# A convolution and a low-rank mixer on one core: the large products in halves of 64 rows

## The chip, the cores and the metric

The kernel runs on one core of a Trainium2 chip. The metric is the device time of one execution in microseconds (us); shorter is better. Engines are named as the profile names them: PE is TensorE's matmul and PEld its weight load, DVE is VectorE, ACT is ScalarE, POOL is GpSimd, SP is SyncE; "q" after a name is that engine's sequencer. L560 is line 560 of the kernel before.

## The reference

`x` is (8, 4224, 192) and `out` has the same shape, float32. The first stage is a causal convolution along the sequence with seven taps for each of eight heads of 24 channels, after a softmax of the taps. The second stage mixes.

```python
w = softmax(weight)                                  # 8 heads x 7 taps
y[b, s, h, :] = sum_k w[h, k] * xpad[b, s + k, h, :]  # x padded with 6 zeros in front
h = (y^T @ U) @ V          # U: 4224 x 32, V: 32 x 4224, along the sequence
u = y + h^T
out = u + relu(u @ w_ch1) @ w_ch2    # 192 -> 768 -> 192
```

`h` needs a whole batch of `y` before the first row of `u`.

## The kernel before, in words

The sequence of a batch is 33 tiles of 128 rows, and all batches together 264 tiles; 33 groups of eight tiles go through the mixer, one group a round. Data is bfloat16, sums in PSUM are float32.

**Convolution** (`conv_two`, L355). A 128 x 128 band matrix per head multiplies blocks of tiles, two heads into the two banks of one PSUM buffer, and ScalarE or VectorE copies them to `y_sb`. A second band brings the last rows of the tile before; batches 0 and 1 use both bands. From batch 2 on only the first band is used, and the first six rows of each tile come from `conv_halo` (L381): POOL loads the rows around each tile border (`load_halo`, L92), eight matmuls make the six rows, ScalarE copies them, and two DMAs on SP bring them to `y_sb` by way of DRAM (`put_halo`, L408).

**Low rank** (`low_rank`, L414). 33 matmuls of 32 columns of `U` each sum `y^T U` of a batch in four groups of 32 partitions; VectorE copies the sums out. `fold` (L434) is a float32 matmul (two passes) that adds the four groups and leaves the result in two places; VectorE copies it to `tt_sb`. `mix_quad` (L443) multiplies `V` with it for four tiles, lower and upper 64 rows of the array by turns into two banks, and VectorE adds `y_sb` into `u_sb` (L467). `turn_by_dma` (L540) transposes a group of `u_sb` with one DMA on SP into `uT_sb`; for groups 0 and 1 TensorE does it (`straight`, `turn`).

**The mixer's products.** `h1_chunk` (L551) is the first product: 192 channels as three blocks of 64 rows, so lower and upper half of the array hold different tiles and write different banks, six matmuls of 512 columns a chunk, six chunks a group; ScalarE (m = 0, 2, 4, 5) or VectorE (m = 1, 3) applies the relu. `w2_step` (L574) is the second: per tile six matmuls with all 128 rows and 192 columns (L582), a buffer for four tiles; VectorE adds `u_sb` (L593), and SP stores (L600).

**What sets the order.** All instructions stand in the order in which the program writes them, for each engine in its own queue. In round g come some quads of group g + 2, the six chunks of group g, the other quads, and then eight pieces of the second product, the second half of group g - 1 and the first half of group g; `beside` lists what stands after which piece: convolutions of a later batch, the transposing DMA of group g + 2 (after the third piece), `low_rank`, `fold`, the loads of a batch two ahead at a round's end. One pool of four PSUM buffers of two banks, `big`, serves all of it in turn.

The lines that need to be seen:

```python
quads = [(g + AHEAD, 0)], [(g + AHEAD, QT)]
for q in quads[0]: mix_quad(*q)
for m in range(MC): h1_chunk(g, m)
for q in quads[1]: mix_quad(*q)
...
gg, n0 = (g - 1, W2N // 2) if i < NP // 2 else (g, -W2N // 2)
```

Of the kernel before, what the change touches and what calls it, by code (L numbers as in the profile page):

```python
# [15 lines left out]
def kernel(  # L16
# [41 lines left out]
    hxs = ctx.enter_context(tc.tile_pool(name="hxs", bufs=2))  # L58
# [9 lines left out]
    big_ps = ctx.enter_context(tc.tile_pool(name="big_ps", bufs=4, space=bass.MemoryType.PSUM))  # L68

    def big(dtype=F32):  # L70
        return big_ps.tile([P, 2, BK * 4 // mybir.dt.size(dtype)], dtype, name="big")
# [4 lines left out]
    x_tiles, hx_tiles = {}, {}  # L76
    blocks_0 = [(0, 8), (8, 16), (16, 24), (24, 30), (30, NT)]
    assert blocks_0[0][1] >= GT
    blocks = [(s, min(s + CB, NT)) for s in range(0, NT, CB)]
# [12 lines left out]
    def load_halo(b):  # L92

        hx = hxs.tile([HJ * HP, HS, D], BF16, name="hx_sb")
        for s in range(HS):
            src = x[b, (s + 1) * P - HALO, :]
            nc.gpsimd.dma_start(  # L97
                out=hx[:, s, :],
                in_=bass.AP(src.tensor, src.offset, [[D, HP], [HS * P * D, HJ], [1, D]]),
            )  # L100
        hx_tiles[b] = hx
# [67 lines left out]
    halo_band = cst.tile([HJ * HP, H, P], BF16, name="halo_band")  # L169
# [5 lines left out]
    idle_ps = big()  # L175
# [31 lines left out]
    def keep_busy(n):  # L207
# [19 lines left out]
        in_=ident[0 : HJ * HP, 0:1].to_broadcast([HJ * HP, H * P]),  # L227
# [55 lines left out]
    nc.vector.memset(V_sb[:, 0 : S // 2].bitcast(U32), 0)  # L283

    fold_sb = cst.tile([P, P], F32, name="fold_sb")
    nc.gpsimd.memset(fold_sb[:], 0.0)
    id4 = ident[:].rearrange("p (q r) -> p q r", r=R)
    f2 = cst.tile([P, 2, R], F32, name="f2")
    nc.gpsimd.tensor_tensor(out=f2[:], in0=id4[:, 0:2, :], in1=id4[:, 2:4, :], op=ALU.add)
    for h in range(2):  # L290
        nc.gpsimd.tensor_tensor(
            out=fold_sb[:, h * HB : h * HB + R], in0=f2[:, 0, :], in1=f2[:, 1, :], op=ALU.add
        )
# [21 lines left out]
    def build_halo_band():  # L315
        cps = big()
        for c in range(HALO):
# [8 lines left out]
            out=halo_band[:, :, 0 : HALO * HJ].rearrange("p h (c j) -> p h c j", j=HJ),  # L326
# [9 lines left out]

    def load_others():
        first = GT * P
        nc.gpsimd.dma_start(out=V_sb[0:R, 0:first], in_=moe_V[:, 0:first])
# [5 lines left out]
        nc.gpsimd.dma_start(out=V_sb[0:R, first:], in_=moe_V[:, first:])  # L345
        nc.gpsimd.dma_start(out=V_sb[HB : HB + R, :], in_=moe_V[:])
# [6 lines left out]
    y_tiles, tps_tiles, tt_tiles, u_tiles, ut_tiles = {}, {}, {}, {}, {}  # L353
# [372 lines left out]
```

## Time and profile before

| What | Value |
|---|---|
| Runs | 342.75, 346.08 and 346.15 us, median 346.08 |
| The profiled execution | 343.05 us, of which the profile's span is 341.2 |
| TensorE granted clock | 1.000 |
| First chunk of round 0 begins | 21.82 us |
| First chunks of rounds 1, 2, 3 and 4 begin | 31.00, 47.37, 60.19 and 69.73 us |
| Last matmul of the second product ends | 337.28 us |
| First product L560 | 1188 matmuls, 133.8 us busy, 376 ns one |
| Second product L582 | 1584 matmuls, 148.6 us busy, 246 ns one |
| Its weight loads | 1584, 98 ns one |
| Relu on ScalarE L570, on VectorE L572 | 132 by 1022 ns, 66 by 1218 ns |
| o_sb on VectorE L593 | 67 by 946 ns |
| u_sb on VectorE L467 | 128 by 549 ns |

How to read it: matmuls are pipelined, so the length of one (246 ns) is longer than the distance between two starts. The chain of waits is followed back from the last instruction to what released each; a piece of it on PE is a stretch in which TensorE's own order sets the time. "Idle before" with a releaser tells what ended a wait.

### The profile page before, as it was taken

To read this page: it belongs to the slowest core of one execution; us is meant where nothing else is said; L and a number is where in the kernel's file an instruction comes from. 1 tells how busy PE (TensorE), PEld (TensorE's weight loads), DVE (VectorE), ACT (ScalarE), POOL (GpSimd) and SP (SyncE) were. 2 spreads that over 40 slices of the span, in tenths; PEclk is the share of its full clock that TensorE was granted. 3 is DMA by queue.
4 is the path that set the end of the run, shared out by engine and by line. 5 is a ranking of instruction groups with operands and counts; after the bars stand their busy time and mean duration, and the time that the engine had idled before them with its cause. 6 is when DMAs were issued, how large, how long until landed. Compare 5 with 4: busy or idle time off the path is not lost.

```text
span 341.2 us, 8411 instructions
## 1 busy us (share of the span) xinstructions
PE 329.2 (96%) x3663; PEld 232.8 (68%) x3663; DVE 224.2 (66%) x323; ACT 193.1 (57%) x220; POOL 43.7 (13%) x70
## 2 busy tenths in 40 slices
PE   4998998999999999999999999999999999999995
PEld 2856666666677777766676777776677767777775
DVE  6758574667666556776766656667677767777553
ACT  5456647676555756666555745685565434444550
POOL 7680050050005000140005000000000000000000
PEclk9999999999999999999999999999999999999999
DMA  8999999999955996599947997535247444464424
GB/s 127 198 197 193 180 151 164 221 186 192 231 162 119 200 210 174 99 207 167 255 140 134 205 200 158 170 102 161 95 138 149 140 140 138 140 140 140 139 95 138
DMA packets 122965, 55.40 MB, mean 162 GB/s; under 512 B 88266, under 2 KB 122730, under 8 KB 122794
## 3 DMA queue, kind: packets, MB, share of 16 engines
q1 hardware_dynamic: 83988, 39.31, 48.4%
q0 software_dynamic: 38896, 15.29, 37.8%
q8 instruction: 28, 0.46, 0.5%
q10 hardware_dynamic: 44, 0.27, 0.3%
q14 instruction: 9, 0.07, 0.1%
HBM read 31.56 MB, written 26.39 MB: 170 GB/s over the span
## 4 chain that ended last, share of the span: by engine, by line
PE 90%; DMA 6%; ACT 1%; DVE 1%; issue 0%; POOLq 0%
PE big L582 38%; PE big L560 36%; PE big L365 8%; PE big L455 4%; DMA uT_sb<-u_sb 4%; DMA x_sb<-in_x_dram 2%; PE big L422 2%; PE big L436 1%; PE big L192 1%; ACT rl_sb L570 1%; PE big L388 1%; DVE o_sb L593 0%; DVE u_sb L467 0%; ACT uT_sb L537 0%; PE big L526 0%
## 5 line engine op out<-in xcount | busy, mean ns | idle before, releaser
L570 ACT ACTIVATE rl_sb<-big 128x1024 bf16<-128x1024 f32 x132 | 131.6, 1022 | 92.0 <-DVE o_sb L593 35.6
L582 PE MATMUL big<-W_sb,rl_sb 128*128 128x192 bf16 x1584 | 148.6, 246 | 0.0
L582 PEld LDWEIGHTS <-rl_sb 128*128 128x128 bf16 x1584 | 130.4, 98 | 14.4 <-issue 5.7
L560 PE MATMUL big<-uT_sb,W_sb 64*128 64x512 bf16 x1188 | 133.8, 376 | 2.0 <-DMA uT_sb<-u_sb 1.4
L593 DVE TENSOR_TENSOR o_sb<-big,u_sb 128x768 f32<-128x768 f32 (+1 forms) x67 | 63.4, 946 | 84.3 <-PE big L582 84.3
L560 PEld LDWEIGHTS <-W_sb 64*128 64x128 bf16 x1188 | 58.2, 94 | 64.8 <-DVE u_sb L467 6.8
L572 DVE TENSOR_SCALAR rl_sb<-big 128x1024 bf16<-128x1024 f32 x66 | 78.1, 1218 | 4.0 <-PE big L560 3.6
L375 ACT ACTIVATE y_sb<-big 128x1008 bf16<-128x1008 f32 (+4 forms) x64 | 48.8, 769 | 36.5 <-PE big L365 35.8
L467 DVE TENSOR_TENSOR u_sb<-y_sb,big 128x384 bf16<-128x384 bf16 x128 | 64.8, 549 | 5.5 <-PE big L455 5.4
L87 POOL DMA_DIRECT2D x_sb<-in_x_dram x19 | 21.8, 1153 | 139.4 <-PE big L365 138.2
L365 PE MATMUL big<-x_sb,band_sb 128*128 128x504 bf16 (+4 forms) x208 | 38.0, 302 | 1.0 <-DMA x_sb<-in_x_dram 0.9
L455 PE MATMUL big<-tt_sb,V_sb 64*128 64x192 bf16 x264 | 22.1, 245 | 1.0 <-ACT rl_sb L570 0.6
L365 PEld LDWEIGHTS <-band_sb 128*128 128x128 bf16 x208 | 18.3, 101 | 3.0 <-ACT U_sb L203 1.0
L455 PEld LDWEIGHTS <-V_sb 64*128 64x128 bf16 x264 | 10.5, 94 | 13.6 <-issue 6.4
L97 POOL DMA_DIRECT2D hx_sb<-in_x_dram x24 | 13.7, 577 | 0.0
L377 DVE CAST y_sb<-big 128x384 bf16<-128x384 f32 (+4 forms) x12 | 6.8, 570 | 4.5 <-PE big L365 4.1
L440 DVE CAST tt_sb<-big 128x192 bf16<-128x192 f32 x8 | 2.9, 357 | 9.4 <-PE big L436 9.4
L422 PE MATMUL big<-y_sb,U_sb 128*32 128x192 bf16 x264 | 7.7, 252 | 0.0
L422 PEld LDWEIGHTS <-U_sb 128*32 128x32 bf16 x264 | 6.2, 139 | 1.2 <-issue 1.1
L397 ACT ACTIVATE hy_sb<-big 48x384 bf16<-48x384 f32 x12 | 5.2, 478 | 2.6 <-PE big L388 2.6
L436 PE MATMUL big<-tf_sb,fold_sb 128*128 128x192 f32 x16 | 4.3, 348 | 0.2 <-DVE tf_sb L431 0.2
L209 PE MATMUL big<-ident 128*128 128x512 bf16 x3 | 1.6, 617 | 2.8 <-POOL ident L129 2.8
(68 smaller groups left out, 53.2 us busy)
## 6 DMA issues: line engine op xcount, KB each, us to landing
out_dram<-o_sb SPq DMA_DIRECT2D x65, 384.0 KB, 3.3
x_sb<-in_x_dram POOLq DMA_DIRECT2D x7, 1008.0 KB, 13.4
x_sb<-in_x_dram POOLq DMA_DIRECT2D x7, 576.0 KB, 17.3
x_sb<-in_x_dram POOLq DMA_DIRECT2D x3, 384.0 KB, 7.5
W_sb<-in_moe_w_ch_dram POOLq DMA_DIRECT2D x3, 288.0 KB, 7.6
hx_sb<-in_x_dram POOLq DMA_DIRECT2D x24, 36.0 KB, 16.9
uT_sb<-u_sb SPq DMA_TRANSPOSE x31, 4.0
hy_dr<-hy_sb SPq DMA_DIRECT2D x6, 72.0 KB
```

What stands on the lines that cost most here:

```text
L87: nc.gpsimd.dma_start(out=x_tiles[b][:, 1 + s0 : 1 + s1, :], in_=x[b, s0 * P : s1 * P, :].rearrange("(j p) d -> p j d", p=P),)
L97: nc.gpsimd.dma_start(out=hx[:, s, :], in_=bass.AP(src.tensor, src.offset, [[D, HP], [HS * P * D, HJ], [1, D]]),)
L365: nc.tensor.matmul(out=cps[:, q, 0:n], lhsT=band_sb[:, hh + q, w, :], rhs=x_sb[:, 1 + s0 - w : 1 + s1 - w, hc], start=(w == 0), stop=(w == ...
L375: nc.scalar.activation(out=dst, in_=src, func=ACT.Copy)
L422: nc.tensor.matmul(out=tps[q * R : (q + 1) * R, 0, 0:D], lhsT=U_sb[:, :, j], rhs=y_sb[:, j, :], start=(j < n), stop=(j >= NT - n),)
L455: nc.tensor.matmul(out=ups[:, t, i * D : (i + 1) * D], lhsT=V_sb[rows, j * P : (j + 1) * P], rhs=tt_tiles[b][rows, :], start=True, stop=True,)
L467: nc.vector.tensor_tensor(out=dst, in0=y_tiles[b][:, j : j + 2, :].rearrange("p t (k r) -> p t k r", r=HB), in1=add, op=ALU.add,)
L560: nc.tensor.matmul(out=h1[:, q, :], lhsT=W1_sb[rows, k, m * P : (m + 1) * P], rhs=ut[rows, k, :, :], start=(k == 0), stop=(k == KB - 1),)
L570: nc.scalar.activation(out=rl, in_=src, func=ACT.Relu)
L572: nc.vector.tensor_scalar_max(out=rl, in0=src, scalar1=0.0)
L582: nc.tensor.matmul(out=ch[:, t % w, 0:D], lhsT=rl_tiles[g][:, m, t, :], rhs=W2_sb[:, m, :], start=(m == 0), stop=(m == MC - 1),)
L593: nc.vector.tensor_tensor(out=o_sb[:, 0:w, :].rearrange("p t (k r) -> p t k r", r=HB), in0=ch[:, 0:w, 0:D].rearrange("p t (k r) -> p t k r ...
```

## The change

**Halves.** A new class issues a product as two groups of sums in two banks of one buffer, in two parts. In the first part the lower 64 rows of the array work for bank 0 and the upper 64 for bank 1; in the second part they change banks. Each whole matmul becomes two with half the rows, in pairs. The second part may begin when the last two matmuls of the first have ended: a `nop` on POOL waits for these two, and the first two matmuls of the second part wait for that `nop`.

**Where it is used.** The second product (`w2_parts`), the convolutions from batch 1 on (`conv_parts`), and the halo matmuls (`halo_parts`, now with 128 rows of which 32 are zero). The last group's second product stays whole (`w2_whole`). `low_rank` stays at 128 rows. The second product of a group runs wholly in the next round, in two halves of four tiles, each from one buffer of a pool of its own (`ch_ps`, one buffer); `big` keeps three.

**No fold.** VectorE copies the upper 64 partitions of the low-rank sums and adds the lower 64 to them twice, once for each half of `tt_sb`; two of the four groups remain to be added, and `V_sb` holds `V` in all four groups of 32 partitions, so the product with `V` adds them. For group 0 the four groups are used as they are. V is loaded four times over, by POOL and one copy on SP.

**Other moves.** Batch 1 uses one band and a halo like the later ones. Blocks of x are 17 and 16 tiles (21 and 12 before). x of a batch is loaded in two steps of one round, its halo in two steps of the next.

**The order.** Each round follows a word: x0, x1 are quads of group g + 2; m0 to m5 chunks; P0 and Q0 the first and second part of the second product's first four tiles, P1 and Q1 of the others; c and d first and second parts of convolutions; h and H of the halo; L is `low_rank`, t the transposing DMA, l0 and l1 loads, s `put_halo`, y other quads, u another transposing DMA, T a transpose on TensorE, b the halo's band.

```diff
-    big_ps = ctx.enter_context(tc.tile_pool(name="big_ps", bufs=4, space=bass.MemoryType.PSUM))
+    big_ps = ctx.enter_context(tc.tile_pool(name="big_ps", bufs=3, space=bass.MemoryType.PSUM))
+    ch_ps = ctx.enter_context(tc.tile_pool(name="ch_ps", bufs=1, space=bass.MemoryType.PSUM))
...
-    blocks = [(s, min(s + CB, NT)) for s in range(0, NT, CB)]
+    blocks = [(0, (NT + 1) // 2), ((NT + 1) // 2, NT)]
...
+        def V_rows(c0, c1, n):
+            return bass.AP(moe_V.tensor, moe_V.offset + c0, [[0, n], [S, R], [1, c1 - c0]])
+        nc.gpsimd.dma_start(out=V_sb[:, 0:V1], in_=V_rows(0, V1, P // R))
...
+        nc.gpsimd.dma_start(out=V_sb[0:HB, V1:], in_=V_rows(V1, S, HB // R))
+        nc.sync.dma_start(out=V_sb[HB:, V1:], in_=V_sb[0:HB, V1:])
...
+    class Halves:
+        def __init__(self, items):
+            self.items = items
+        def part(self, second):
+            N = len(self.items[0])
+            last = []
+            for n in range(N):
+                for h, rows in enumerate((lower, upper)):
+                    out_, lhsT, rhs = self.items[h ^ second][n]
+                    mm = nc.tensor.matmul(
+                        out=out_,
+                        lhsT=lhsT[rows],
+                        rhs=rhs[rows],
+                        start=not second and n == 0,
+                        stop=bool(second) and n == N - 1,
+                    )
+                    if not second and n == N - 1:
+                        last.append(mm.ins)
+                    elif second and n == 0:
+                        tc.add_manual_dep(mm.ins, self.seen.name, SYNC, reason="a bank changes hands")
+            if not second:
+                self.seen = nc.gpsimd.nop().ins
+                for ins in last:
+                    tc.add_manual_dep(self.seen, ins.name, SYNC, reason="a bank changes hands")
...
-    def fold(b):
-        tps = tps_tiles[b]
-        nc.tensor.matmul(
-            out=tps[:, 1, 0:D], lhsT=fold_sb[:], rhs=tt_tiles[b][:], start=True, stop=True
-        )
...
+            if b == 0:
+                part = tfs.tile([P, D], BF16, name="part_sb")
+                nc.vector.tensor_copy(out=part[:], in_=tps[:, 0, 0:D])
+                part_tiles[b] = part
+            tf = tfs.tile([HB, D], F32, name="tf_sb")
+            nc.vector.tensor_copy(out=tf[:], in_=tps[HB:, 0, 0:D])
+            tt = tts.tile([P, D], BF16, name="tt_sb")
+            for h in range(2):
+                nc.vector.tensor_tensor(
+                    out=tt[h * HB : (h + 1) * HB, :], in0=tps[0:HB, 0, 0:D], in1=tf[:], op=ALU.add
+                )
...
+            ch = big(pool=ch_ps)
+            state["ch"] = ch[:].rearrange("p h (t w) -> p (h t) w", t=QT)[:, :, 0:D]
+            state["mm"] = Halves(
+                [
+                    [
+                        (
+                            ch[:, q, i * (BK // QT) : i * (BK // QT) + D],
+                            rl_tiles[g][:, m, t0 + q * QT + i, :],
+                            W2_sb[:, m, :],
+                        )
+                        for i in range(QT)
+                        for m in range(MC)
+                    ]
+                    for q in range(2)
+                ]
+            )
...
+    USUAL = "x0 m0 m1 P0 c0 m2 d0 c1 l0 Q0 d1 m3 s m4 L x1 t P1 m5 h l1 Q1 H"
+    ORDERS = {
+        0: "m0 y0 m1 y1 m2 m3 T m4 x0 m5 x1 t b",
+        1: "y0 m0 y1 m1 P0 c0 m2 d0 c1 Q0 d1 x0 m3 c2 m4 d2 P1 x1 t c3 m5 d3 c4 h Q1 H d4",
+        2: "m0 m1 P0 c0 m2 d0 c1 Q0 d1 m3 c2 m4 d2 s P1 c3 m5 Q1 d3 L",
+        3: "y0 y1 u m0 m1 P0 c0 m2 d0 c1 l0 Q0 d1 x0 m3 m4 x1 t P1 c2 m5 d2 c3 h l1 Q1 H d3",
+        4: "x0 m0 m1 P0 c0 m2 d0 c1 l0 Q0 d1 m3 m4 x1 t P1 c2 l1 m5 d2 s Q1",
+    }
...
+        last = (nb * NT) // GT - AHEAD - 1
+        if nb == 1:
+            last, shares = 2, {1: 5, 2: 3}
+        elif nb == 2:
+            shares = {2: 1, 3: 4, 4: 3}
+        else:
+            shares = {g: 2 for g in range(last - 4, last)}
...
+        for m in range(MC):
+            on_act = m not in ((2, 4, 5) if len(conv_by[g]) > 2 else (2, 4))
+            if g == 0:
+                on_act = m != 4
...
+    w2_whole(NG - 1, 0, HT, ch_ps)
+    w2_whole(NG - 1, HT, QT, big_ps)
+    w2_whole(NG - 1, HT + QT, QT, big_ps)
```

In rounds from 5 to 24 each round has two convolutions; x of batches 3 to 7 is loaded in rounds 3, 5, 9, 13 and 17, and `low_rank` of batches 1 to 7 stands in rounds 2, 5, 9, 13, 17, 21 and 25.

## The prediction

> **What bounds the kernel now.** First the page: busy shares, clock and DMA rows, and the chain that ended last.
>
> ```profile
> span 341.2 us, 8411 instructions
> PE 329.2 (96%) x3663; PEld 232.8 (68%) x3663; DVE 224.2 (66%) x323; ACT 193.1 (57%) x220; POOL 43.7 (13%) x70
> ...
> PEclk9999999999999999999999999999999999999999
> DMA  8999999999955996599947997535247444464424
> ...
> PE 90%; DMA 6%; ACT 1%; DVE 1%; issue 0%; POOLq 0%
> PE big L582 38%; PE big L560 36%; PE big L365 8%; PE big L455 4%; DMA uT_sb<-u_sb 4%; DMA x_sb<-in_x_dram 2%; PE big L422 2%; PE big L436 1%; PE big L192 1%; ACT rl_sb L570 1%; PE big L388 1%; DVE o_sb L593 0%; DVE u_sb L467 0%; ACT uT_sb L537 0%; PE big L526 0%
> ```
>
> TensorE's order of work is the time, at full clock. The DMA engines are as full in the first third, and one DMA is on the chain. So two questions: what in TensorE's order is not streaming, and which DMAs does it wait for? Next the chain in one round, in order of time (start, length, what):
>
> ```profile
> 89.63 0.27 PE big L455 x4
> 89.90 3.89 PE big L560 x36
> 93.79 0.17 PE big L455 x4
> 93.95 1.59 PE big L582 x18
> 95.55 0.24 PE big L365 x2
> 95.79 0.99 PE big L582 x12
> ```
>
> L560 streams: 18 pairs in 3.89 is 0.216 a pair. L582 streams at 0.99/12 = 0.0825. Four L455 after L560 (both in halves of 64 rows) take 0.17; after L582 (128 rows) 0.27, so that joint costs 0.105. Eighteen L582 should take 1.485 and take 1.59 after L455: 0.105 again. L365 to L582, both 128 rows, costs nothing. Then the timeline, for halves at 192 columns and for the late DMA:
>
> ```profile
> 89.56 0.12 PEld L455 LDWEIGHTS <-V_sb 64*128 64x128 bf16 x4 [0.16 <-issue]
> 89.57 0.34 PE L455 MATMUL big<-tt_sb,V_sb 64*128 64x192 bf16 x4
> 89.66 1.69 PEld L560 LDWEIGHTS <-W_sb 64*128 64x128 bf16 x18
> 89.74 4.05 PE L560 MATMUL big<-uT_sb,W_sb 64*128 64x512 bf16 x36
> ```
>
> ```profile
> 48.17 3.87 SPq L542 DMA_TRANSPOSE uT_sb<-u_sb  x1
> 60.19 4.06 PE L560 MATMUL big<-uT_sb,W_sb 64*128 64x512 bf16 x36 [1.42 <-DMA uT_sb<-u_sb]
> ```
>
> Four half matmuls start at 89.57 and the next at 89.74: two pairs in 0.17, 0.083 a pair, as fast as one whole matmul. The transposing DMA issued at 48.17 landed 12.0 later and TensorE stood 1.42. Its landing while x was loading, and with the queues empty (windows at 114 and 132 us):
>
> ```profile
> DMA to landing us min/median/max: 10.6/10.6/10.6
> ```
> ```profile
> DMA to landing us min/median/max: 3.2/3.2/3.2
> ```
>
> **The sum** is made against the profiled execution: span 341.2, own time 343.05, so 1.85 lies around it. That time is 0.9% below the median of the runs (346.08).
>
> *Removed or saved.*
> Joints: 2 x 0.105 in each of about 32 rounds, 6.7; the last group stays whole and keeps 0.2: -6.5. L422 stays at 128 rows and keeps its joints (0.89 + 0.11 a batch).
> The second product: 1,536 whole matmuls at 0.0825 become 1,536 pairs. Bounds from rows: 0.083 (L455) and 0.094 (one half's LDWEIGHTS lasts 94 ns, if it could not hide), 0 to +18. I take 0, since L582 hides a 98 ns load in 82.5 already.
> First convolutions: two matmuls of 408 columns by 0.17 either way (L365: 504 columns, 0.21 each): 0. Batch 1 gets one band instead of two: in the chain 5.4 become 2.7, its halo adds 0.34: -2.3.
> Halo in halves: 8 pairs for 8 matmuls, 0.34 a batch; if loads limit it 0.66, so 0 to +2.2; taken 0.
> Fold (L436): 0.35 in seven batches, 2.45; in the prologue, fold and tt_sb are out of the way of L504: -0.7 (L422 ends 19.17, three L488 groups until 20.05, L504 then instead of at 20.73). Together -3.2. VectorE instead makes one copy and two adds by 0.36 a batch; they stand in its queue before the next u_sb adds, counted below.
> The 1.42 wait at 60.19: that transpose now has a round and a half more: -1.4.
> V_sb's two memsets (0.94 each on VectorE) go: they lay beside the first convolutions, and a convolution copy may start sooner: 0.
> Sum: -13.4.
>
> *Added.* One round by hand, a round with low_rank and halo, from x0 = 0, with 0.165 a quad, 0.65 a chunk, 0.99 a part, 0.17 a convolution half: m0 to 0.81, m1 1.46, P0 2.45, c0 2.62, m2 3.27, d0, c1 3.61, Q0 4.60, d1, m3, m4 6.07, L 7.07, x1 7.23, P1 8.2, m5 8.9, h 9.1, Q1 10.1, H 10.3. VectorE: m2 until 4.75, o_sb 5.82, m4 7.55, L's three 8.63, x1's adds 9.7.
> Three PSUM buffers instead of four (the fourth is ch): h's buffer is read by ScalarE (2 x 0.48) from 10.5 to 11.45, and the next round's m1 wants it at 11.1: 0.38 x 6 batches, +2.3. Only one ch: in the eight rounds without convolutions P1 wants it at 5.55, when VectorE gives it up (2 o_sb by 0.96 and m2 by 1.22): +0.5. All other turns of the three buffers have 0.2 or more to spare.
> Round 0: ScalarE has five chunks by 1.02; buffers come back late at y1, m3, m5 and x1, by hand 2.45 of idle against some 1.6 now: +0.9. Batch 1: low_rank ends round 2 and y0 needs its tt_sb; three VectorE steps, 1.3 of idle against 1.0: +0.3. Round 1 has VectorE busy 9.6 of 10.6, and POOL, whose loads wait for landings of earlier ones, may hold the first bank changes until x of batch 1 has landed (31.2 now): 0.5 to 2.5, taken 1.5.
> POOL's own queue: batch 1's halo adds four issues by 0.57; x (1.05 to 1.45) and halo loads are now spread between steps, behind the nops that matter. SP: same stores, one copy of V more, under the prologue.
>
> *The wait at a bank change* (127 of them). TensorE's last matmul ends, POOL's nop sees it, the second part may start. Behind the waiting matmul stands all of TensorE. Cover: one chunk, 0.65, at the least. Of it 0.48 is left after the last matmul's end (0.65 + 0.08 - 0.25), less a weight load of 0.1: 0.38. Price: a matmul's end to ScalarE's start 0.04 (L365 to L375), VectorE's end to TensorE 0.05 (L440 to L455), a POOL instruction after the one it waits for 0.07 (L305): some 0.15. Far end: POOL's loads start 0.23 to 0.67 after L436 or L365 ended. [...] With 0.67 + 0.08 each exposed wait costs 0.37, and 63 have only a chunk as cover: +23. A wait added to a bound engine can't gain.
>
> *The transposing DMA.* Now it is issued 5.2 us into a round (95.08 against 89.90) and needed two rounds later. After the change it stands behind m4 and x1 on VectorE: issued at 9.75 of the round above, needed at 10.3 + 0.4 + 8.9 + 0.2 = 19.7: 9.95. In rounds 5, 9, 13 and 17 x loads run beside it: the first half issued at 3.95, the second at 9.4. Rows beside x loads: 10.6, 10.7, 11.5, 12.0; alone 3.2. All contended: 0.65 to 2.05 late. But the second half of x is issued only then, and a gap opens before it; the nearest row, 10.6, less some of that: I take 0.5 late, five times (round 3 too): +2.5; ends 0 and +10.
>
> Added: 2.3 + 0.5 + 0.9 + 0.3 + 1.5 + 2.5 = 8.0. Net -5.4: 337.6 in the profiled execution's terms. The runs lie up to 3.1 above that execution; I put the time at 339.0, some 1.4 up.
>
> [...] By the trace a switch between 128 and 64 rows costs 0.105, both ways. [...] By the trace four half loads start within 0.03 us and pairs follow at 0.083. [...] The rows do not show them one at a time.
>
> **Rivals.**
> (a) The sum: 337.6, own range 334 to 342. Chance 0.42.
> (b) The transposes land in time: 335 (337.6 - 2.5). For: 3.2 alone, and loads are spread. Against: every transpose beside x needed over 10. 0.22.
> (c) They are late by the worst row, 2.05 five times: +7.7, 345. For: 12.0 at 48.17. Against: the gap between the halves. 0.14.
> (d) Slower: the way through POOL outlasts the chunk. 63 exposed waits; at the far end 361. It decides from 0.54 instead of 0.38 on: 63 x 0.14 = 8.8 takes the net -5.4 to +3.4, 1%. For: POOL's 0.67. Against: every other hand-over is under 0.1. 0.14, near 350 on average.
> (e) Pairs at 0.094: 355. Against: L455. 0.08.
> That the halves don't do what they say, and the joints stay, would add 6.5 to (a), 344; the joint-free L365 to L582 speaks against; it is part of (c)'s chance.
>
> **How the numbers follow.** About 1% is what a measurement of this kernel can tell from no change: 339.6 to 346.5 in own terms. Faster: (b) 0.22 and most of (a), 0.36: 0.58. Same: the rest of (a), 0.06, and (c): 0.20. Slower: (d) and (e): 0.22. Range: from (b) with half the other stalls gone, 331, to the middle of (d), 350; beyond lies (e) and half of (d), and a little below: under 0.2.
>
> **What would show it.** Joints: the chain shows L560, quads and the second product with no step above 0.17 a quad, and parts of 24 halves in 0.99. Bank changes: no idle of TensorE put down to POOL. h: ScalarE's hy_sb ends idle before a first product's chunk, 0.4 in six rounds. Transposes: idle put down to the DMA into uT_sb in rounds 7, 11, 15 and 19. Waits after each second part would prove (d); parts of 1.1 us (e).

## The result and the profile after

The changed kernel takes 369.45 us (median of four runs, 368.15 to 378.89) against 346.0 of the kernel before: a ratio of 1.068, with an interval of 1.061 to 1.076. It is slower by 6.8%, where 339 was forecast. The run of 378.89 was disturbed and is left out of the ratio. The profiled execution took 368.68 us, of which 366.9 are its span.

The page of the kernel after, the same rows as were shown of before:

```profile
span 366.9 us, 11937 instructions
PE 326.5 (89%) x5343; PEld 243.9 (66%) x5343; DVE 231.1 (63%) x334; ACT 189.7 (52%) x221; POOL 44.8 (12%) x69
...
PE   4970488978979999988999999899999999999994
...
PEclk9995599999999999999999999999999999999999
DMA  8998996339999954999499949996445556544533
...
PE 59%; DMA 14%; DVE 2%; issue 1%; ACT 0%; ACTq 0%; DVEq 0%; SPq 0%
```

TensorE is busy for a little less time than before (326.5 us against 329.2), in a span that is 25.7 longer. The row PE has a hole from the third to the fifth slice (18 to 46 us), empty in the fourth, and in the fourth and fifth the granted clock is 5 tenths. DMAs hold 14% of the chain, where they held 6; this chain reaches back only to 89 us, so round 0 is not on it. So the products did not get slower; TensorE waits, and first of all in round 0.

The chain in a round well behind these first ones, with two convolutions, to be set beside the round shown of before (start, length, what):

```profile
116.61 1.29 PE big L642 x12
117.90 0.17 PE big L537 x4
118.07 0.99 PE big L374 x24
119.06 0.65 PE big L642 x6
119.70 0.99 PE big L374 x24
120.69 0.16 PE big L537 x4
```

A part of the second product (24 halves) takes 0.99, a chunk 0.65, a quad 0.16 or 0.17 behind a chunk and behind the second product alike. The steps of 0.105 that stood beside L582 in the kernel before are gone, and nothing waits for a bank. (Behind `low_rank`, still of 128 rows, a quad takes 0.27.) This is what the prediction drew. Now round 0, in the timeline of the kernel after:

```profile
24.38 1.23 PE L642 MATMUL big<-uT_sb,W_sb 64*128 64x512 bf16 x6 [0.26 <-ACT uT_sb L597]
34.29 0.54 SPq L344 DMA_DIRECT2D V_sb<-V_sb  x1
34.32 0.34 PE L537 MATMUL big<-tt_sb,V_sb 64*128 64x192 bf16 x1 [8.72 <-DMA V_sb<-in_moe_V_dram]
34.83 2.49 POOL L88 DMA_DIRECT2D x_sb<-in_x_dram  x2 [9.51 <-DMA V_sb<-in_moe_V_dram]
41.33 0.50 PE L537 MATMUL big<-tt_sb,V_sb 64*128 64x192 bf16 x3 [6.67 <-DMA V_sb<-V_sb]
```

The first quad waits 8.72 us for the load of V's rest, its next matmul 6.67 more for SP's copy of the same rows into the upper 64 partitions, which could only start when the load had landed (34.29). POOL's own next loads of x stand 9.51 us behind the same load. What this does to the clock is in the windows of the kernel after (stretch, length, busy time of each engine, granted clock, DMA share, GB/s):

```profile
20.00:25.30 5.30, 4.58 (x91) 3.28 (x88) 3.41 (x9) 2.17 (x6) 1.68 (x3) 1.00 1.93 156
25.30:34.30 9.00, 0.30 (x4) 0.00 (x0) 0.53 (x2) 1.02 (x1) 0.01 (x1) 0.63 1.10 139
34.30:41.40 7.10, 0.41 (x3) 0.18 (x5) 0.00 (x0) 0.00 (x0) 2.48 (x2) 0.50 1.01 137
41.40:45.00 3.60, 3.60 (x24) 2.55 (x25) 2.04 (x4) 1.28 (x2) 0.59 (x1) 0.54 1.60 192
```

TensorE is idle here from 25.61, and in the trace's own list its clock is 0.5 from 27.65 to 44.72: the windows show 0.63 and 0.50 in the wait, and the next 3.6 us of work run at 0.54. Later, the chain passes the halo rows of batch 2, which go through DRAM, while x of batch 3 is loading (its last block lands at 102.4):

```profile
89.70 10.85 DMA hy_dr<-hy_sb
100.60 6.75 DMA y_sb<-hy_dr
107.39 0.89 PE big L503 x32
```

**Where the time went.** For every matmul the trace has its start, and how long it streams; what lies between two starts beyond that is a wait. The waits of the profiled executions add up as in the table; beside them stand the time lost to the granted clock (busy time in windows of 4 us by one less the clock that the windows show, where it is under 1), and the time from the first convolution to the first low-rank matmul, less the waits in it. The last column is the span less these three: work that TensorE streams, joints included, and the two ends of the span.

| Kernel | span | waits | clock | convolutions of batch 0 | the rest |
|---|---|---|---|---|---|
| before | 341.2 | 7.5 | 0.0 | 9.2 | 324.5 |
| after | 366.9 | 40.0 | 1.9 | 12.7 | 312.4 |

The change took 12.1 us out of the work and put 32.5 into waits: V 15.7; the transposing DMAs 4.1 (1.6 before); the halo rows 3.6; u_sb of VectorE 3.4, y_sb of ScalarE 2.9, o_sb of VectorE 2.8, hy_sb 2.6 (PSUM buffers that these four free late); the rest small. The 3.5 of the fifth column will be shown not to belong to the change.

### The profile page after: what moved, and what is told of

The parts are those of the page before. It is cut to its first block, busy times and chain, and to the rows that moved or that the text cites. A ratio compares the mean times of both kernels' runs of the same rounds, so it can differ in the third digit from the quotient of the medians.

```text
span 366.9 us, 11937 instructions
## 1 busy us (share of the span) xinstructions
PE 326.5 (89%) x5343; PEld 243.9 (66%) x5343; DVE 231.1 (63%) x334; ACT 189.7 (52%) x221; POOL 44.8 (12%) x69
## 4 chain that ended last, share of the span: by engine, by line
PE 59%; DMA 14%; DVE 2%; issue 1%; ACT 0%; ACTq 0%; DVEq 0%; SPq 0%
PE big L374 29%; PE big L642 25%; DMA uT_sb<-u_sb 9%; DMA hy_dr<-hy_sb 3%; PE big L537 2%; DMA y_sb<-hy_dr 2%; DVE o_sb L661 2%; PE big L503 1%; PE big L709 1%; ACT y_sb L413 0%; ACT hy_sb L474 0%; DVE rl_sb L654 0%; ACTq L652 0%; DVEq L654 0%; SPq L490 0%
## 5 line engine op out<-in xcount | busy, mean ns | idle before, releaser
L642 PE MATMUL big<-uT_sb,W_sb 64*128 64x512 bf16 x1188 | 155.4, 379 | 8.5 <-DMA uT_sb<-u_sb 3.6
L374 PE MATMUL big<-W_sb,rl_sb 64*128 64x192 bf16 x3072 | 149.1, 243 | 0.3 <-DVE o_sb L661 0.3
L374 PEld LDWEIGHTS <-rl_sb 64*128 64x128 bf16 x3072 | 132.3, 94 | 17.8 <-issue 0.9
L654 DVE TENSOR_SCALAR rl_sb<-big 128x1024 bf16<-128x1024 f32 x69 | 84.5, 1225 | 72.1 <-PE big L642 71.1
L413 ACT ACTIVATE y_sb<-big 128x816 bf16<-128x816 f32 (+4 forms) x66 | 50.8, 770 | 46.5 <-PE big L374 37.7
L374 PE MATMUL big<-x_sb,band_sb 64*128 64x408 bf16 (+1 forms) x224 | 34.2, 328 | 0.3
L374 PEld LDWEIGHTS <-band_sb 64*128 64x128 bf16 x224 | 12.6, 94 | 7.1 <-DVE u_sb L549 0.9
L399 PE MATMUL big<-x_sb,band_sb 128*128 128x192 bf16 (+2 forms) x80 | 10.9, 328 | 0.8 <-DMA x_sb<-in_x_dram 0.8
L399 PEld LDWEIGHTS <-band_sb 128*128 128x128 bf16 x80 | 9.6, 141 | 1.6 <-ACT U_sb L207 0.9
L520 DVE TENSOR_TENSOR tt_sb<-big,tf_sb 64x192 bf16<-64x192 f32 x16 | 5.6, 350 | 0.4
```

The costliest lines, as they stand in the source:

```text
L374: mm = nc.tensor.matmul(out=out_, lhsT=lhsT[rows], rhs=rhs[rows], start=not second and n == 0, stop=bool(second) and n == N - 1,)
L399: nc.tensor.matmul(out=cps[:, q, 0:n], lhsT=band_sb[:, hh + q, w, :], rhs=x_tiles[b][:, 1 + s0 - w : 1 + s1 - w, hc], start=(w == 0), stop ...
L413: nc.scalar.activation(out=dst, in_=src, func=ACT.Copy)
L642: nc.tensor.matmul(out=h1[:, q, :], lhsT=W1_sb[rows, k, m * P : (m + 1) * P], rhs=ut[rows, k, :, :], start=(k == 0), stop=(k == KB - 1),)
L654: nc.vector.tensor_scalar_max(out=rl, in0=src, scalar1=0.0)
```

## The experiments

My theory was that the load of V, as it is written, is the main cost: one DMA whose source repeats V's 32 rows by an outer step of zero. That the form makes it slow was an estimate, from the landing at 34.27 us. In transfers of 32 rows I expected V's rest by 14, TensorE's two waits in round 0 (the first for the load, the second for SP's copy) under 2 us together, no cut of the clock behind them, and 351 to 355 for the kernel. Rivals: the bytes (V four times over), SP's copy alone, or loads that collide whatever form V has. Ratios are to the kernel before, with their intervals.

**V by groups of 32 rows.**

```diff
-        nc.gpsimd.dma_start(out=V_sb[:, 0:V1], in_=V_rows(0, V1, P // R))
+        for n in range(P // R):
+            nc.gpsimd.dma_start(out=V_sb[n * R : (n + 1) * R, 0:V1], in_=moe_V[:, 0:V1])
...
-        nc.gpsimd.dma_start(out=V_sb[0:HB, V1:], in_=V_rows(V1, S, HB // R))
+        for n in range(HB // R):
+            nc.gpsimd.dma_start(out=V_sb[n * R : (n + 1) * R, V1:], in_=moe_V[:, V1:])
```

> The kernel after, with only the load of V written differently: instead of one transfer whose source repeats V's 32 rows by an outer step of zero (4 x 32 rows, then 2 x 32), one transfer for every group of 32 rows (four, then two); bytes, queue and SP's copy stay. [...] Rival 1, the bytes (V is read four times over, 0.8 MB in place of 0.5): the load still lands after 25 us, time 366 or more. Rival 2, SP's copy from SBUF to SBUF is slow whatever comes before it (6.99 us): the first wait goes, the second stays, about 360.

Measured: 365.77, ratio 1.055 (1.050 to 1.061), where 351 to 355 was expected. The transfers are quicker, the time hardly. V's rest lands at 22.5 us instead of 34.27, but not by 14: its two transfers are issued at 14.8 and 15.5, and their packets begin at 17.5. From issue to landing of V's transfers in this kernel (13.7, 19.6 and 25.5 in the kernel after):

```profile
DMA to landing us min/median/max: 5.7/7.9/8.7
```

The wait for the load is gone and 3.5 us are left behind SP's copy, as rival 2 had it in part; V's 15.7 have become 3.5. But other waits and the clock took most of it back. Groups of the kernel with V by rows:

```profile
L644 PE MATMUL big<-uT_sb,W_sb 64*128 64x512 bf16 x1188 | 158.0, 384 | 9.6 <-DMA uT_sb<-u_sb 5.7 <-DVE u_sb L551 1.1 <-ACT hy_sb L476 0.6
L505 PE MATMUL big<-y_sb,U_sb 128*32 128x192 bf16 x264 | 8.7, 266 | 5.0 <-DMA y_sb<-hy_dr 4.7 <-ACT y_sb L415 0.4
```

and its windows:

```profile
96.00:100.00 4.00, 0.23 (x3) 0.07 (x2) 1.23 (x1) 0.52 (x1) 0.00 (x0) 0.95 1.29 234
100.00:104.00 4.00, 3.85 (x66) 3.18 (x67) 2.08 (x5) 0.00 (x0) 0.00 (x0) 0.62 1.41 222
164.00:168.00 4.00, 3.63 (x28) 2.24 (x30) 0.02 (x1) 1.93 (x2) 0.00 (x0) 0.57 1.17 231
```

TensorE reaches the halo rows and the transposed tiles earlier, and these have not come earlier: from 3.6 to 5.0 and from 4.1 to 6.6 us of waits, and behind two of them (4.1 us before 100, 2.3 before 164.4) the clock is cut to some 0.6. Behind SP's copy it is cut too (half from 27.95 to 34.78). In all the clock costs 7.2 us here, against 1.9.

**The same load with the dimensions exchanged.**

```diff
-            return bass.AP(moe_V.tensor, moe_V.offset + c0, [[0, n], [S, R], [1, c1 - c0]])
+            return bass.AP(moe_V.tensor, moe_V.offset + c0, [[S, R], [0, n], [1, c1 - c0]])
```

> The kernel after, with the two outer dimensions of V's source exchanged (32 rows outside, the repeat of 4 or 2 inside): still one transfer for each piece, same bytes, the same steps of zero, only the slowest dimension is now 32. The rows of V land in another order, so the part of the output that V adds is not the reference's; shapes and work are the same. [...] If the step of zero itself (the same rows read again) or the bytes are what is slow, it stays at 366 or more.

Measured: 361.21, ratio 1.045 (1.041 to 1.050), 8.2 us below the kernel after and again not the 351 to 355 of the theory. The landings, to be set beside 13.7, 19.6 and 25.5:

```profile
DMA to landing us min/median/max: 9.8/11.6/13.3
```

Not all of the 8.2 is the line's. The profiled spans differ by 6.9: 4.6 less of waits, 1.0 more of clock, and 3.7 of a quicker start, which other kernels with the same convolutions show or lack too (below). What the line itself does is shown by the packets. The load of V's rest is 64 packets of 6,400 bytes in both kernels, some 0.5 us each by the trace. In the kernel after they come with 2.0 in flight on the mean, over 17.0 us; here with 8.5 in flight, over 3.7; by groups of rows with 9.0, over 3.5. A packet takes as long (0.52 and 0.50 us), from the same bytes and with the same step of zero: what differs is how many are on their way at once. Why the one form has fewer than the other no run shows. SP's copy still cost 6.7 us of waiting: that rival holds for its own part.

**V's new load alone, in the kernel before.** Its V load is replaced by the change's, all else stays.

```diff
-        nc.gpsimd.dma_start(out=V_sb[0:R, 0:first], in_=moe_V[:, 0:first])
+        nc.gpsimd.dma_start(out=V_sb[:, 0:first], in_=V_rows(0, first, P // R))
...
-        nc.gpsimd.dma_start(out=V_sb[0:R, first:], in_=moe_V[:, first:])
-        nc.gpsimd.dma_start(out=V_sb[HB : HB + R, :], in_=moe_V[:])
+        nc.gpsimd.dma_start(out=V_sb[0:HB, first:], in_=V_rows(first, S, HB // R))
+        nc.sync.dma_start(out=V_sb[HB:, first:], in_=V_sb[0:HB, first:])
```

> The kernel before, with only the change's load of V (one transfer with an outer repeat of 4, one with 2, and SP's copy for the upper 64 rows) in place of its own three transfers; all products as they were. If V's load is the change's main cost, this alone puts 10 to 16 us on the kernel before: 356 to 362. If the load is only late because of what else the change starts in its first 30 us, it stays within 3 us of the kernel before, 346 to 349.

Measured: 358.86, ratio 1.039 (1.035 to 1.044): 13.0 us from this alone. In the view of V_sb of this kernel, who waited for it and the landings:

```profile
PEld L459: 12.0, 2
PE big L459: 11.3, 2
...
DMA to landing us min/median/max: 10.3/15.7/21.2
```

The matmuls of the first quad wait 11.3 us (for the load and for SP's copy), as the weight loads ahead of them do. The load is slow without anything else of the change.

**The second product whole, at the same places** (with V by groups of rows).

```diff
+        def whole(q):
+            ch = state["raw"]
+            for i in range(QT):
+                for m in range(MC):
+                    nc.tensor.matmul(
+                        out=ch[:, q, i * (BK // QT) : i * (BK // QT) + D],
+                        lhsT=rl_tiles[g][:, m, t0 + q * QT + i, :],
+                        rhs=W2_sb[:, m, :],
+                        start=(m == 0),
+                        stop=(m == MC - 1),
+                    )
...
-            state["mm"].part(1)
+            whole(1)
```

> The kernel after with V loaded by groups of 32 rows, and the second product made in whole matmuls of 128 rows at the same four places of each round, so that no bank changes hands there; all joints between products of 64 and of 128 rows come back. My step of the prediction: 0.105 us for every joint, 8 a round, 32 rounds, so 27 us above the same kernel with halves: 378 to 382. Rival: joints cost nothing when other work stands there, and what the halves saved was only the waits: within 5 us of the kernel with halves.

Measured: 376.89, ratio 1.088 (1.082 to 1.095), so 11 us above the kernel with V by rows and not 27. The chain shows the joints in full:

```profile
292.44 0.17 PE big L539 x4
292.61 1.10 PE big L684 x12
293.70 0.75 PE big L644 x6
294.46 1.10 PE big L684 x12
295.55 0.27 PE big L539 x4
```

1.10 for 0.99, 0.75 for 0.65, 0.27 for 0.17: a joint costs 0.105. The two spans differ by 13.4: the work by 26.9 more, the waits by 10.3 less (the slower rounds leave the transposing DMAs and the halo rows time to land), the clock by 2.9 and the start by 0.3 less. Eight joints by 0.105 in 32 rounds are 26.9. So the size of the joints was right, and two things were hidden from one total: late DMAs give back to a slower TensorE what they take from a quicker one.

**Loads out of each other's way.** All of V by groups of rows (SP's copy left out), x of batches 4 to 7 in eight pieces over four rounds and of batch 3 in four over two, the last second product begun in the free pool.

```diff
-            for n in range(2):
-                steps[g][f"l{n}"] = lambda b=b, n=n: (
+            N = 4 if nb == 1 else 8
+            for n in range(N):
+                steps[g + n // 2][f"l{n % 2}"] = lambda b=b, n=n, N=N: (
                     new_x(b) if n == 0 else None,
-                    load_x(b, *blocks[n]),
+                    load_x(b, n * NT // N, (n + 1) * NT // N),
+                    load_halo(b, 0, HS // 2) if n == N - 3 else None,
+                    load_halo(b, HS // 2, HS) if n == N - 2 else None,
                 )
-                steps[g + 1][f"l{n}"] = lambda b=b, n=n: load_halo(b, n * HS // 2, (n + 1) * HS // 2)
...
-    w2_whole(NG - 1, 0, HT, ch_ps)
-    w2_whole(NG - 1, HT, QT, big_ps)
+    w2_whole(NG - 1, 0, HT, big_ps)
+    w2_whole(NG - 1, HT, QT, ch_ps)
```

> The kernel after with V read from DRAM by groups of 32 rows for all 128 partitions (eight transfers, SP's copy left out), x's loads for batches 3 to 7 in eight pieces over four rounds (batch 3: four pieces over two) in place of two pieces in one round, and the last second product begun in the free PSUM pool. Theory: what is left above the forecast is loads that fall on other transfers, with the clock's cut behind the longer waits. V's wait (3.5 us with V by rows) goes under 0.5, the transposing DMA's four waits (6.4 together) under 1, the wait for the halo rows (5 together) to about 2, the two waits of the tail (1.7) to about 0.7, the clock's loss (7.2) under 3: 365.8 less about 16, so 347 to 353. Rival: the same bytes take the same share of the DMA engines whenever they come, pieces only move the waits to the convolutions, which then wait for x: 360 or more.

Measured: 346.27, ratio 1.005 (1.001 to 1.008): 23 us below the kernel after, level with the one before. The page's rows and the chain:

```profile
span 344.6 us, 11984 instructions
...
PEclk9999999999999999999999999999999999999999
DMA  8999993399999999999899999999445544445534
...
PE 73%; DMA 2%; DVE 2%; issue 1%; ACT 0%; ACTq 0%; DVEq 0%
```

The DMA engines are full from a fifth of the span to seven tenths of it, and yet DMAs hold 2% of the chain (which reaches back to 73 us). V's waits, the transposing DMAs' and the clock's loss behind waits are all zero; the halo rows still cost 3.8. How long SP's queue takes to issue a transposing DMA (ns, shortest, median, longest) shows what the pieces did, here first with V by rows, then with x spread:

```profile
L626 SPq DMA_TRANSPOSE uT_sb<-u_sb x31: 1329/1417/6687, 39.1 to 338.4; - x31
```
```profile
L625 SPq DMA_TRANSPOSE uT_sb<-u_sb x31: 1386/1406/2577, 33.8 to 319.9; - x31
```

The longest issue with V by rows, 6.7 us at 151.2, stands beside the second half of a batch's x (issued at 142.1, landed at 160.6). With x spread the longest, 2.6 at 33.8, stands beside x of batches 1 and 2, which is not spread; beside an eighth none is over 1.8. The three edits were made at once; the trace tells them apart, not the total.

**No cover for the bank change.** The same kernel with each second part of the second product right behind its first.

```diff
+            if step[0] == "Q":
+                continue
             if step in steps[g]:
                 steps[g].pop(step)()
+            if step[0] == "P" and g > 0:
+                steps[g].pop("Q" + step[1])()
```

> The kernel f1_spread with the second part of every second product issued right behind its first part, so that no chunk, convolution or mixing stands between them while the bank changes hands (64 places). If the way from TensorE through POOL and back is what the prediction's rival (d) took it for, each place now shows an idle TensorE in front of the second part: at 0.15 to 0.4 us each 10 to 26 us, so 358 to 376, and a way of 0.54 or more (34 us) would have outlasted the chunk of 0.65 in the kernel after. If the way costs under 0.05 us, the time is that of f1_spread within 3 us, and the cover is not needed.

Measured: 395.06, ratio 1.145 (1.139 to 1.151): 49 above the kernel it was made from, more than the way alone can cost. Now the way shows in front of the weight loads (timeline, and the group that these belong to):

```profile
289.94 0.61 PEld L375 LDWEIGHTS <-rl_sb 64*128 64x128 bf16 x14
290.88 0.94 PEld L375 LDWEIGHTS <-rl_sb 64*128 64x128 bf16 x24 [0.33 <-POOLq L387]
```
```profile
L375 PEld LDWEIGHTS <-rl_sb 64*128 64x128 bf16 x3072 | 126.1, 94 | 29.0 <-POOLq L387 21.5
```

TensorE's waits that POOL's nop ends are 95 (64 of the second product, the others of convolutions that lost their cover too), 0.27 each and 26.1 together. In the second product the second part starts 0.351 after the last start of the first; a half lasts 0.243, so some 0.11 lies between its end and the next start. Most of the rest are ScalarE's evictions (26.5 of waiting for them, where 3.4 was): chunks now stand side by side and fill three buffers faster than 1.02 us an eviction empties them. The chunk between the parts covers the way and the buffers at once.

**Whole products where loads are spread.** The edit of whole products again, in the kernel with x spread.

> The kernel f1_spread with the second product whole, in products of 128 rows at the same places. With V by rows alone whole products cost 11 us, not the 27 that 0.105 us for a joint makes of 8 joints in each of 32 rounds; by the traces because the slower rounds let the transposing DMAs and the halo rows come in time (10 us of waits and 3 of clock less). Where the loads are spread, little is left to give back: 346.3 and 22 to 27, so 368 to 373. Rival: what the joints cost lies under other waits here too, and it stays at 11: 357.

Measured: 370.82, ratio 1.072 (1.067 to 1.078): 24.5 above, as the theory had it. In the profiles the work is 26.8 more and the waits are the same, 19.5: with the DMAs in time nothing gives the joints back.

**TensorE's start.** The fifth column of the table differs by 3.5 us between kernels that issue the same convolutions. The timelines of the kernel after and of the one with V's dimensions exchanged:

```profile
12.25 2.74 PE L399 MATMUL big<-x_sb,band_sb 128*128 128x192 bf16 x16
```
```profile
12.26 1.49 PE L399 MATMUL big<-x_sb,band_sb 128*128 128x192 bf16 x16
```

The same 16 matmuls take 2.74 or 1.49: a matmul of 192 columns every 160 ns or every 82. The quick rate came at 11 us in the profile of the kernel before and at 21 in that of the kernel after. A trace keeps the granted clock as a list of stretches, and a window shows 1.00 for a time that the list does not cover. The list begins, with full clock, at 20.82 us in the kernel after, at 11.80 with V's dimensions exchanged, and at 11.30 in the kernel before, so that the 1.000 ahead of the prediction holds from there on only. In the kernel after, the last matmuls of the convolutions start every 60 ns until 20.8 us and every 33 behind it. In the windows from 12 to 16 us nine of the 14 profiles have 28 to 30 matmuls and five have 43 to 45; two of the nine, both with the filler products named below, show a clock of 0.50 there, all others 1.00. In these windows the kernel after (not covered yet), the kernel before with the filler products named below (covered, at half) and the kernel before (covered, at full) hold 28, 29 and 43 matmuls:

```profile
12.00:16.00 4.00, 4.00 (x28) 3.46 (x28) 1.11 (x2) 1.37 (x3) 2.71 (x3) 1.00 1.42 193
```
```profile
12.00:16.00 4.00, 4.00 (x29) 3.50 (x29) 2.10 (x4) 1.68 (x4) 3.46 (x6) 0.50 1.40 200
```
```profile
12.00:16.00 4.00, 4.00 (x43) 3.76 (x43) 2.71 (x7) 1.74 (x4) 3.08 (x4) 1.00 1.41 199
```

The uncovered start goes at the rate of the one with a clock of 0.50 (28 and 29 matmuls), so the fifth column is a price of the clock too. I tried seven more filler products (`keep_busy`, 128x512 in the profile) in the first 8.6 us, in the kernel with x spread and in the kernel before.

```diff
-    keep_busy(2)
+    keep_busy(5)
...
-    keep_busy(1)
+    keep_busy(3)
...
+    keep_busy(1)
     U_turned = [turn_U(0), turn_U(1)]
...
+    keep_busy(2)
     for n, (s0, s1) in enumerate(blocks_0):
```

> The kernel f1_spread with seven more of the four-column filler products in the places of the first 8.6 us where TensorE waits. Theory: the long half-rate start (a 192-column half product every 160 ns until 20.8 us in the profile of after, until 11.3 us in that of before) comes from TensorE's idle places in the first 8 us, and costs 3.5 us when it is long; filled, the first convolutions run at 82 ns by 11 us at the latest in each run: 2 to 4 us under f1_spread where f1_spread starts slowly, and a spread of its own runs under 1.5 us. Rival: how long the start is at half rate does not depend on TensorE's idle places; within 1 us of f1_spread, with the same spread.

> The kernel before with the same filler products in the same places. Theory: the runs of before fall in two groups (342.8 to 344.3, and 345.8 to 346.5) for the same start at half rate; with the filler all come out at 341 to 344. Rival: the groups have another cause, and the median stays at 346.

Measured: 350.52, ratio 1.015 (1.009 to 1.022), so 4 above and not below the kernel with x spread; and 343.60 for the kernel before, 0.997 (0.993 to 1.002), with its runs still in two groups (341.8 to 344.1, and 345.9 to 346.3). The first expectation failed in an instructive way. The profiled start was quick (82 ns from 9.7 us on, the low-rank product at 18.2 instead of 22.4), and TensorE then met V and the halo rows before they had come. Groups and windows of that kernel:

```profile
L505 PE MATMUL big<-y_sb,U_sb 128*32 128x192 bf16 x264 | 8.7, 266 | 5.6 <-DMA y_sb<-hy_dr 5.2 <-ACT y_sb L415 0.4
```
```profile
60.00:64.00 4.00, 4.00 (x35) 2.91 (x31) 1.90 (x5) 2.05 (x2) 0.00 (x0) 0.50 0.25 57
96.00:100.00 4.00, 4.00 (x56) 3.02 (x52) 1.87 (x5) 0.58 (x1) 0.00 (x0) 0.57 0.26 63
```

It lost 7.1 us to the clock around and behind these waits. The second theory falls: in its profile the kernel before, with filler, ran at the quick rate for three matmuls and then at 160 ns from 9.6 to 19 us, with a granted clock of 0.5. The filler moves the slow stretch and does not end it. With the filler the two groups go with the clock: the three runs at 345.9 to 346.3 have a mean granted clock of 0.985, what a cut of 10.24 us (9.62 to 19.86 in the profile) makes of the span, and the six at 341.8 to 344.1 have 0.993 to 1.000. For the kernel before as it is, that the start makes the two groups is likely by size (3.5 against 3.2 us), not shown, since one of its runs alone left a trace. What decides when the clock rises stays open.

**The order of rounds 0 to 5.** In the kernel with x spread: a fourth buffer in round 0, low-rank of batches 1 and 2 later, quads of round 3 between chunks, half of the halo's copy to DVE.

```diff
-        2: "m0 m1 P0 c0 m2 d0 c1 Q0 d1 m3 c2 m4 d2 s P1 c3 m5 Q1 d3 L",
-        3: "y0 y1 u m0 m1 P0 c0 m2 d0 c1 l0 Q0 d1 x0 m3 m4 x1 t P1 c2 m5 d2 c3 h l1 Q1 H d3",
+        2: "m0 m1 P0 c0 m2 d0 c1 Q0 d1 m3 c2 m4 d2 s P1 c3 m5 Q1 d3",
+        3: "m0 L m1 y0 P0 y1 u c0 m2 d0 c1 l0 Q0 d1 x0 m3 m4 x1 t P1 c2 m5 d2 c3 h l1 Q1 H d3",
+        5: "x0 m0 m1 P0 c0 m2 d0 c1 l0 Q0 d1 m3 s m4 x1 t P1 m5 h l1 L Q1 H",
...
+                if h == 0:
+                    nc.scalar.activation(out=dst, in_=src, func=ACT.Copy)
+                else:
+                    nc.vector.tensor_copy(out=dst, in_=src)
```

> The kernel f1_spread with its own waits taken out of the way in rounds 0 to 5: in round 0 every fourth result goes to the PSUM tile that the second product does not use yet; the low-rank product of batch 1 comes one chunk into round 3 and that of batch 2 at the end of round 5 (both waited for the halo rows, 1.0 and 2.8 us); round 3's mixing stands between chunks; one of the two copies of the halo result goes from ACT to DVE. Theory: what f1_spread still lacks against the forecast is order and buffers in these rounds: of its 19.5 us of waits, the halo rows' 3.8, the 1.2 behind the low-rank product, 2 of round 0's 2.9 and 2 of ACT's 2.6 go, so 8 to 9 us off 346.3: 337 to 339, below the kernel before. Rival: DVE and ACT are what bounds rounds 0 to 4 (their evictions per round, not the order), and the waits come back in front of other products: 343 or more.

> The kernel g1_order with the seven more filler products in the first 8.6 us. f2_warm started quickly (first convolutions at 82 ns, the low-rank product 4.2 us earlier) but met V and the halo rows before they had landed (1.9 and 5.5 us) and lost 7.1 us to the clock behind these waits. With the halo's waits moved the quick start should be kept: 2 to 4 us under g1_order. Rival: the loads set the end of the first 60 us whichever way TensorE starts, and the time is that of g1_order or up to 4 us more.

Measured: 345.27, ratio 0.999 (0.996 to 1.003), and with the filler 345.24, 1.001 (0.998 to 1.005), where 337 to 339 and less were expected. The halo rows' wait went (3.8 to 0.5), and the rival was right about the copy that I moved:

```profile
L647 PE MATMUL big<-uT_sb,W_sb 64*128 64x512 bf16 x1188 | 154.2, 377 | 6.0 <-DVE hy_sb L487 4.2 <-DVE u_sb L554 1.1 <-ACT uT_sb L602 0.3
```

VectorE's copy stands behind a chunk's eviction; 5.3 us of waits in seven places where ScalarE alone had cost 2.6. Undone, with the halo product's two parts ahead of the round's last part:

```diff
-    USUAL = "x0 m0 m1 P0 c0 m2 d0 c1 l0 Q0 d1 m3 s m4 L x1 t P1 m5 h l1 Q1 H"
+    USUAL = "x0 m0 m1 P0 c0 m2 d0 c1 l0 Q0 d1 m3 s m4 L x1 t P1 h m5 H l1 Q1"
...
-            shares = {2: 1, 3: 4, 4: 3}
+            shares = {2: 1, 3: 3, 4: 4}
```

> The kernel g1_order with what its trace shows as its own: the halo result is copied by ACT alone again (in seven places TensorE waited for DVE's half, 0.7 each and 5.3 together, where ACT alone had cost 2.6), both halves of the halo product come before the last second part of the round instead of around it, and one convolution of batch 2 goes from round 3 to round 4. Theory: 5.3 us of these waits and about 1 in round 3 go, nothing comes back: g1_order's 345.3 less 4 to 6, so 339 to 342, about 1% below the kernel before. Rival: ACT's evictions bound these rounds and the waits return under another name: 344 to 346.

Measured: 343.88, ratio 0.995 (0.991 to 0.999): half a per cent below the kernel before, half of what was expected. Its profiled execution, one of its quick starts, has a span of 338.7, with 15.1 us of waits left; 2.3 of them are for V again. It is the only version below both kernels, by little and at the edge of what the runs can tell.

**All profiled executions in one table**, columns as above:

| Kernel | span | waits | clock | convolutions of batch 0 | the rest |
|---|---|---|---|---|---|
| V by groups of rows | 364.0 | 31.7 | 7.2 | 12.7 | 312.5 |
| V, dimensions exchanged | 360.0 | 35.4 | 2.9 | 9.0 | 312.7 |
| before, with V's new load | 356.6 | 18.3 | 1.8 | 12.5 | 324.0 |
| whole second product | 377.4 | 21.4 | 4.2 | 12.4 | 339.4 |
| x spread | 344.6 | 19.5 | 0.0 | 12.7 | 312.4 |
| x spread, whole second product | 369.0 | 19.5 | 1.4 | 9.0 | 339.2 |
| second order of rounds 0 to 5 | 338.7 | 15.1 | 1.5 | 9.0 | 313.1 |

The last column falls into three groups: 324 for the order of before, 312 to 313 for halves, 339 for whole products at the places of the change. Everything else that the runs differ by is waits, clock and start.

## Why the prediction was wrong

- **Joints, fold, batch 1's second band: right in sum.** The prediction had 6.5 + 3.2 + 2.3 = 12.0; the last column has 324.5 less 312.4, 12.1. Of the three the joint alone was measured by itself (0.105).
- **The second product in pairs at 0: right.** 24 halves take 0.99, as 12 whole matmuls did. Rival (e) falls.
- **The bank change at 0: right.** That POOL's nop goes by the short hand-overs (some 0.15) and not by its loads (0.23 to 0.67), so that the chunk hides it, was an estimate with no row of a nop behind it. No wait at a bank change is put down to POOL in the kernel after; uncovered it costs 0.27, with 0.11 after the last matmul's end, and the chunk is 0.65. Rival (d), from 0.54 on, falls.
- **"SP: same stores, one copy of V more, under the prologue": this step failed.** It is the whole price that the prediction gave to V. The load, written with an outer step of zero, had 2.0 packets on their way, landed at 34.27 instead of 21.5, and the copy behind it at 41.3, where the prologue ends at 24.4. 15.7 us of waits, 1.9 of clock behind them; alone in the kernel before it cost 13.0. Landing times of V stood in the trace of before, and the form of the new source in the diff; the step looked at neither. None of the five rivals names V, and (d), the slowest, ended at 361.
- **The halo rows were left out.** Two DMAs through DRAM beside x's loads: 3.6 us in front of the low-rank products of batches 1 and 2, no term in the sum.
- **The transposing DMAs: the mechanism right, the size low.** Taken 0.5 five times, 2.5, ends 0 and 10; measured 4.1 in the kernel after, 6.6 with V by rows, zero with x spread. The signs named rounds 7, 11, 15 and 19; the waits came in 11, 12 and 19. The prediction read one DMA on the chain of before; its row has two, the second x_sb's first 7 us.
- **Buffers: right in kind, low in sum.** h's buffer, 0.38 six times taken, measured 0.30 six times and 0.78 once. Waits for u_sb, y_sb, hy_sb and o_sb together 11.6, where 2.3 + 0.5 + 0.9 + 1.5 = 5.2 stood in the sum (the missing ones in rounds 1 to 3 and in the tail, 1.7, where `w2_whole` takes the single buffer). One of o_sb's, 1.1 at 245.8, may be a transposing DMA's: with V by rows the wait at that place is put down to one.
- **The clock was not in the sum at all.** It took 1.9 behind V's wait, 7.2 in all with V by rows, and made the start of the kernel after 3.5 longer than that of before in the profiles, which is no part of the change.

All in all the removed work came out to within 0.1 us. The sum's added 8.0, less the 1.4 of a transpose, were 6.6 against 32.5 of waits and 1.9 of clock. The difference is 27.8, with the 3.5 of the start 31.3, and the profiled execution lies 31.1 above its forecast (368.7 against 337.6). With the loads repaired the kernel is where the kernel before is, within 0.5%, since its other waits eat the 12 us (19.5 against 7.5).

## What to carry to other kernels

Read a DMA's access pattern before its bytes: a repeat of 2 written as the outer dimension had 2.0 packets on their way and took 17.0 us here, the same bytes with 32 rows outside 3.7; split it, or put the repeat inside. When TensorE's order gets shorter, transfers with little slack can become late together, as the halo rows and the transposed tiles did with V by rows, so check the landing time of each against the new time of need, and add the clock's cut behind a long wait (1.9 us in all in the kernel after, 7.2 with V by rows). Keep work, waits and clock apart when a total surprises: here the work changed exactly as forecast while the total went the other way.

## What the runs showed of the hardware that was not expected

- A load of 64 rows of 6,400 bytes had 2.0 packets in flight with a slowest dimension of 2, and 8.5 with one of 32: 17.0 us against 3.7.
- SP's copy of 64 partitions of 6,400 bytes within SBUF took some 7 us from issue to landing (34.29 to 41.3).
- A transposing DMA's issue on SP's queue took 1.3 to 1.4 us alone and 6.7 beside a load of 768 KB (V by rows, at 151.2).
- After a wait of TensorE of 2.3 us the clock was granted at 0.57 for the next 4 us (V by rows, at 164 us); after one of 2.8 us (x spread, 88.5 to 91.3) it stayed at 1.0. What made the difference is not shown. In the kernel after, TensorE's last matmul ahead of V's wait ended at 25.61 and the clock was halved from 27.65 on; it was full again at 44.72, 3.4 us after TensorE's work had gone on at 41.33. The stretches of its list ahead of the last are 6.83, 17.07 and 320.85 us long: the second is 2.50 times the first, the third 47.0 times.
- The convolutions of batch 0 ran at half rate until the granted clock's first stretch of full clock began, at 11.30 us in the kernel before and at 20.82 in the kernel after (there the step between equal matmuls falls from 60 to 33 ns); the windows show 1.00 ahead of it, where the trace has no entry.
